# A tuned attention kernel: one check of the row sums in the last slots, simpler first loads, and quad 2 treated as any other

## The chip, the cores and the metric

One core of a Trainium2 chip runs the kernel. The metric is the device time of one execution in microseconds (us); the profile's span, from the first to the last instruction, is about 1.7 us shorter. Ratios in this document are computed as the mean time of one kernel's fast runs over the mean time of the other's fast runs of the same rounds, with a 95% interval, so they are not quite the ratios of the medians that stand beside them.

## The reference

```python
B, H, Sq, Sk, D = 16, 32, 192, 1024, 128          # bf16 inputs
scale  = q.shape[-1] ** -0.5
scores = jnp.einsum("bhqd,bhkd->bhqk", q, k) * scale
p      = softmax(scores, axis=-1)
out    = jnp.einsum("bhqk,bhkd->bhqd", p, v)
```

512 heads, each with 192 queries and 1024 keys. A "quad" is four heads; there are 128 quads, and a quad is worked on in three "fills" of the score banks, 384 fills (`NF`) in all.

## The kernel before

Each quad takes one load of K (1 MB), one of V (1 MB) and one of Q (192 KB), issued by SyncE into rings of five buffers. VectorE turns K and Q (the STREAM_TRANSPOSE rows; 0.97 us for one of K with 128x768), GpSimd reorders the turned K ("order", three pieces a quad) and spreads V beside a column of ones ("spread", two halves). TensorE computes a score block (`qk`) and, four fills later, an output block (`pv`). ScalarE takes exponentials, VectorE normalizes (`onorm`). The softmax takes no maximum: the row sums are checked against bounds, and where one is out of bounds everything is computed again on a general path (never here).

The loads at the start, on SyncE (cut):

```python
load_k(0)
e.wait_ge(s_blank, 1)
load_k(1); load_q(e, 1)
load_v(0, 0, 2)                       # half of V0
e.wait_ge(s_qk, PRE + 1)              # fill 0 is done
load_v(0, 2, 3); load_v(0, 3, 4)      # the other half, in two
load_k(2, 0, 8); load_k(2, 8, 16)     # half of K2, in two
e.wait_ge(s_qk, PRE + 2)              # fill 1 is done
load_k(2, 16, 24); load_k(2, 24, 32)
load_q(e, 2)
for n in range(3, NKN):               # V1, K3, Q3, V2, K4, Q4
    load_v(n - 2); load_k(n); load_q(e, n)
... # from here each load waits for its buffer
```

Quad 2 (`HELD = 2`) is treated apart: GpSimd orders its second piece of K before it spreads V1, so VectorE must hold the output block of fill 3 until V1's first half is spread:

```python
# GpSimd
order(3 * x)
if x == HELD: order(3 * x + 1)
if x >= 1:    spread(x - 1, 0); spread(x - 1, 1)
if x != HELD: order(3 * x + 1)
order(3 * x + 2)
# VectorE, end of onorm(s)
if s == 3 * (HELD - 1) - 1:
    ins.then_inc(s_held, 1); dve.wait_ge(s_held, 1)
    dve.wait_ge(s_vp, 2 * HELD - 1)
    dve.sem_inc(s_on, 1)
else:
    ins.then_inc(s_on if s < NF - 2 else s_fin, 1)
```

The check runs four times in the loop, over a quarter of the row sums each, in three parts (clamp, compare, reduce) behind three output steps; the last 24 columns are checked at the very end:

```python
PARTS = (0, NF // 4, NF // 2, 3 * NF // 4, NF - 12)
...
part = s - PARTS[i + 1] - 2
if 0 <= part < 3: check(i, part)
```

At the very end SyncE waits for the stores of all ten output buffers.

## Time and profile before

| | before |
|---|---|
| time, three runs | 813.84 us median, 812.44 to 814.58 |
| span of the profiled run | 810.3 us |
| TensorE busy | 799.4 us, 99% |
| ScalarE, VectorE, GpSimd busy | 93%, 74%, 68% |
| fill 0 starts, last fill starts | 8.75 us, 800.50 us |
| moved by the loads and stores | 319 MB, 394 GB/s on the mean |

In a timeline line stand the start and the duration in us, the engine, the source line, the operation with what it writes and reads, the shapes, how many were merged, and in brackets how long the engine idled before and what ended that. "issue" is a stop for which the profile shows no reason. PE is TensorE, DVE VectorE, ACT ScalarE, POOL GpSimd, SP SyncE. The lines that carry the argument stand in the prediction.

### The profile page before, as it was taken

The page shows a single profiled execution, that of the slowest core. Times are in us where ns is not written, and L with a number is a line of the kernel's source. Part 1 is how long each engine was busy: PE and PEld are TensorE (multiplying, and loading weights), DVE is VectorE, ACT ScalarE, POOL GpSimd, SP SyncE. Part 2 cuts the span into 40 slices and gives each one's busy share as a digit, 9 for nine tenths or more (in the row PEclk, how much of TensorE's full clock was granted, in tenths as well). Part 3 has the DMA queues.
Part 4 walks back from the last instruction along what each step waited for, and adds up shares of the span by engine and source line. Part 5 has one row for each costly group of instructions (what it writes and reads, how often), then busy time and mean ns, then how long its engine had stood idle before and what let it go on. Part 6 is the DMA issues. An engine that isn't in the chain of part 4 may idle for free. (4 is left out here: it accounts for less than half of the span.)

```text
span 810.3 us, 71469 instructions
## 1 busy us (share of the span) xinstructions
PE 799.4 (99%) x32996; PEld 713.3 (88%) x32996; DVE 602.5 (74%) x1301; ACT 749.9 (93%) x772; POOL 552.0 (68%) x648
## 2 busy tenths in 40 slices
PE   7999999999999999999999999999999999999998
PEld 5888888888888888888888888888888888888887
DVE  4677777777777777777777777777777777777775
ACT  5999999999999999999999999999999999999996
POOL 5676676677667667766766776676676667766763
PEclk9999999999999999999999999999999999999999
DMA  8999999999999999999999999999999999999994
GB/s 286 405 399 401 402 402 404 409 405 404 408 405 405 407 407 405 404 408 406 404 407 406 404 408 407 403 409 405 404 407 392 407 408 390 403 407 403 391 368 152
DMA packets 138904, 319.17 MB, mean 394 GB/s; under 512 B 7408, under 2 KB 56560, under 8 KB 122608
## 3 DMA queue, kind: packets, MB, share of 16 engines
q1 hardware_dynamic: 108048, 295.79, 93.3%
q10 hardware_dynamic: 30816, 23.01, 8.5%
q14 instruction: 34, 0.28, 0.1%
q8 instruction: 6, 0.10, 0.0%
HBM read 293.60 MB, written 25.17 MB: 393 GB/s over the span
## 5 line engine op out<-in xcount | busy, mean ns | idle before, releaser
L892 ACT ACTIVATE f_pt<-f_s 128x1536 bf16<-128x1536 f32 x384 | 554.6, 1444 | 0.0
L639 POOL COPY f_kt<-f_kx 128x768 uint32<-128x768 uint32 (+1 forms) x384 | 302.2, 788 | 240.3 <-DVE f_kx L783 240.1
L689 PE MATMUL f_s<-f_qt,f_kt 32*128 32x192 bf16 (+1 forms) x20528 | 422.0, 226 | 5.4 <-PEq L672 2.9
L718 PE MATMUL f_o<-f_vp,f_pt 128*64 128x129 bf16 x12368 | 425.9, 222 | 0.9 <-issue 0.9
L718 PEld LDWEIGHTS f_o<-f_vp,f_pt 128*64 128x64 bf16 x12368 | 362.4, 110 | 50.0 <-issue 23.0
L689 PEld LDWEIGHTS f_s<-f_qt,f_kt 32*128 32x128 bf16 x20528 | 348.0, 92 | 41.8 <-issue 6.5
L783 DVE STREAM_TRANSPOSE f_kx<-f_kn 128x768 uint32<-128x768 uint32 (+1 forms) x384 | 333.7, 870 | 9.3 <-DMA f_kn<-in_k_dram 9.1
L889 ACT ACTIVATE f_pt<-f_s 128x512 bf16<-128x512 f32 x384 | 229.3, 597 | 52.5 <-PE f_s L689 9.1
L648 POOL COPY f_vp<-f_vs 128x1024 uint32<-128x1024 uint32 x256 | 260.0, 1046 | 7.8 <-DMA f_vs<-in_v_dram 6.3
L821 DVE RECIPROCAL f_rinv<-f_o 128x2 f32<-128x2 f32 x381 | 64.7, 170 | 180.3 <-PE f_o L718 180.3
L827 DVE TENSOR_TENSOR f_ob<-f_o,f_rinv 128x256 bf16<-128x256 f32 x381 | 161.7, 424 | 13.0
L792 DVE STREAM_TRANSPOSE f_qt<-f_qn 128x384 uint32<-128x384 uint32 x128 | 72.8, 569 | 0.0
L876 ACT ACTIVATE f_pt<-f_ones 128x1536 f32<-128x1536 bf16 x3 | 4.2, 1471 | 0.0
L803 DVE TENSOR_SCALAR f_chk<-f_rinv 128x192 f32<-128x192 f32 (+2 forms) x5 | 3.9, 781 | 0.0
L627 POOL MEMSET f_vp<- 128x1088 uint32 (+1 forms) x3 | 3.8, 1311 | 0.0
L718 PE MATMUL f_s<-f_vp,f_pt 128*64 128x129 bf16 x96 | 3.1, 220 | 0.1
L718 PEld LDWEIGHTS f_s<-f_vp,f_pt 128*64 128x64 bf16 x96 | 2.8, 110 | 0.3 <-ACT f_pt L892 0.3
L805 DVE TENSOR_TENSOR f_chk<-f_chk,f_rinv 128x192 f32<-128x192 f32 (+1 forms) x4 | 2.8, 702 | 0.0
L876 ACT ACT_TABLE_LOAD x1 | 1.3, 1283 | 1.2 <-PEq L922 1.2
L731 PE MATMUL f_o<-f_ones 128*128 128x512 bf16 x2 | 1.0, 618 | 1.1 <-POOL f_ones L624 1.1
L756 DVE MEMSET f_pt<- 128x256 uint32 x4 | 1.1, 272 | 0.9 <-PEq L922 0.9
L821 DVE RECIPROCAL f_rinv<-f_s 128x2 f32<-128x2 f32 x3 | 0.5, 171 | 1.2 <-PE f_s L718 1.2
(16 smaller groups left out, 5.3 us busy)
## 6 DMA issues: line engine op xcount, KB each, us to landing
f_kn<-in_k_dram SPq DMA_DIRECT2D x127, 1024.0 KB, 17.9
f_vs<-in_v_dram SPq DMA_DIRECT2D x127, 1024.0 KB, 16.1
f_qn<-in_q_dram SPq DMA_DIRECT2D x127, 192.0 KB, 14.1
out_dram<-f_ob ACTq DMA_DIRECT2D x55, 384.0 KB, 9.5
out_dram<-f_ob SPq DMA_DIRECT2D x11, 192.0 KB, 5.7
out_dram<-f_ob ACTq DMA_DIRECT2D x6, 192.0 KB, 2.5
f_kn<-in_k_dram SPq DMA_DIRECT2D x4, 256.0 KB, 4.2
f_vs<-in_v_dram SPq DMA_DIRECT2D x1, 512.0 KB, 8.0
```

Of the source, the lines that this page charges most:

```text
L639: gp.tensor_copy(kt[:, x % NKT].bitcast(U32).rearrange("p U (j s u) c -> p U j s (u c)", s=2, u=2)[:, lo:hi], kx[:, x % 2].rearrange("p (U ...
L648: gp.tensor_copy(vp[:, x % NVP, 2 * T * i: 2 * T * i + 2 * T, 0:D].bitcast(U32), vs[:, x % NVS, 2 * i: 2 * i + 2, :].rearrange("p a (t d) ...
L689: ins = pe.matmul(S[:, c0: c0 + n1 - n0], kt[r, x % NKT, 2 * t + h, :, c], qt[r, x % R, h, n0:n1, c], start=w == 0 and g == 0, stop=w == 3 ...
L718: ins = pe.matmul(O[64 * z: 64 * z + 64, u, 0:129], pt[:, x % R, 2 * y + z, t * SQ + 64 * j: t * SQ + 64 * j + 64], vp[:, x % NVP, (2 * y ...
L783: dve.transpose(kx[:, x % 2].rearrange("p (U s j u) -> p s u U j", s=2, j=32, u=2)[:, :, :, lo:hi], kn[:, x % NKN].rearrange("p (s u U i) ...
L792: dve.transpose(qt[:, x % R].bitcast(U32).rearrange("p b (y j u) c -> p u y b (j c)", y=3, u=2), qn[:, x % NKN].rearrange("p (u y b i) -> ...
L803: ins = dve.tensor_scalar(c, rinv[:, lo:hi], 1.0 / RS_HI, 1.0 / RS_LO, ALU.max, ALU.min)
L821: dve.reciprocal(ri, O[:, :, 128]).then_inc(s_rc, 1)
L827: ins = dve.tensor_tensor(ob[:, so, 6 * a + 2 * w: 6 * a + 2 * w + 2, :], O[:, :, 0:128], ri.unsqueeze(2).to_broadcast([128, 2, D]), ALU.mult,
L876: return act.activation(part.bitcast(F32), ones[:, 0:1].to_broadcast([128, 2 * T * SQ // 2]), ACT_FN.Copy)
L889: act.activation(pt[:, x % R, 0, c], s1_ps[:], ACT_FN.Exp, scale=scale).then_inc(s_e1, 1)
L892: act.activation(pt[:, x % R, 1:4, c], s3_ps[f % 2][:], ACT_FN.Exp, scale=scale).then_inc(s_e3, 1)
```

## The change

The intent: take the four checks out of the loop, where each costs TensorE 0.42 to 0.45 us, and put one check between the last output steps; load with fewer and whole transfers (V0 without a wait, K2 behind fill 0, everything from Q2 and V1 on behind fill 2); and drop the special treatment of quad 2. Five of the ten waits for stores also move ahead of the last part of the program.

```diff
-    HELD = 2
-    PARTS = (0, NF // 4, NF // 2, 3 * NF // 4, NF - 12)
+    PARTS = (0, NF - 12)
 ...
+            late = [i % NSO for i in range(len(stores) - 5, len(stores))]
 ...
-                load_v(0, 0, 2)
+                load_v(0)
                 e.wait_ge(s_qk, PRE + 1)
-                load_v(0, 2, 3)
-                load_v(0, 3, 4)
-                load_k(2, 0, 8)
-                load_k(2, 8, 16)
-                e.wait_ge(s_qk, PRE + 2)
-                load_k(2, 16, 24)
-                load_k(2, 24, 32)
+                load_k(2)
+                e.wait_ge(s_qk, PRE + 3)
                 load_q(e, 2)
 ...
+                stored(e, [so for so in range(NSO) if so not in late])   # SyncE, ahead; the late ones as before at the end
 ...
-                    if x == HELD:
-                        order(3 * x + 1)
                     if x >= 1:
                         for i in range(2):
                             spread(x - 1, i)
                     if x < NQ:
-                        if x != HELD:
-                            order(3 * x + 1)
+                        order(3 * x + 1)
                         order(3 * x + 2)
 ...
-                    if s == 3 * (HELD - 1) - 1:
-                        ... # the hold
-                    else:
-                        ins.then_inc(s_on if s < NF - 2 else s_fin, 1)
+                    ins.then_inc(s_on if s < NF - 2 else s_fin, 1)
 ...
-                            part = s - PARTS[i + 1] - 2
+                            part = s - (NF - 5)
```

More of the change, by code (lines that the diff above doesn't have):

```diff
@@ L28, in _only_if, with _general_path @@
     return wrap
-def _general_path(nc, q, k, v, out, redo, hints, stored, G=16, NS=2, LAGS=(2, 4, 5, 7), ROUTES=(R_W, R_W, R_EA)):
+def _general_path(nc, q, k, v, out, redo, hints, stored, stored_late, G=16, NS=2, LAGS=(2, 4, 5, 7), ROUTES=(R_W, R_W, R_EA)):
     B, H, SQ, D = q.shape
@@ L195, in _ @@
             sync_general(e)
-            stored(e)
+            stored_late(e)
         @block.gpsimd
@@ L483, in _attention_kernel @@
         s_fin = sem("f_fin")
-        s_held = sem("f_held")
         s_fl = sem("f_fl")
@@ L567, in hint, with stored @@
                 hints[eng.engine] = eng.mark_branch_hint_location()
+            late = [i % NSO for i in range(len(stores) - 5, len(stores))]
+            def stored(e, sos=range(NSO)):
+                for so in sos:
+                    e.wait_ge(s_st[so], landed(so, len(stores)))
             @block.sync
@@ L617, in _ @@
                         store(e, i)
-            def stored(e):
-                for so in range(NSO):
-                    e.wait_ge(s_st[so], landed(so, len(stores)))
+                stored(e, [so for so in range(NSO) if so not in late])
             @block.gpsimd
@@ L645, in spread @@
                     if i == 0:
-                        gp.wait_ge(s_v[x % NVS], 16 * (x // NVS + (3 if x % NVS == 0 else 1)))
+                        gp.wait_ge(s_v[x % NVS], 16 * (x // NVS + 1))
                         gp.wait_ge(s_pv, 3 * (x - NVP) + 3 + BLANK)
@@ L779, in turn_k @@
                     if b == 0:
-                        dve.wait_ge(s_kn[x % NKN], 16 * (x // NKN + (4 if x % NKN == 2 else 1)))
+                        dve.wait_ge(s_kn[x % NKN], 16 * (x // NKN + 1))
                     if x >= 2:
@@ L832, in onorm @@
                     )
-                    if s == 3 * (HELD - 1) - 1:
-                        ins.then_inc(s_held, 1)
-                        dve.wait_ge(s_held, 1)
-                        dve.wait_ge(s_vp, 2 * HELD - 1)
-                        dve.sem_inc(s_on, 1)
-                    else:
-                        ins.then_inc(s_on if s < NF - 2 else s_fin, 1)
+                    ins.then_inc(s_on if s < NF - 2 else s_fin, 1)
                 turn_k(0)
@@ L896, in _ @@
                     store(act, i)
-        _general_path(nc, q, k, v, out, redo, hints, stored)
+        _general_path(nc, q, k, v, out, redo, hints, stored, lambda e: stored(e, late))
 def bass_standalone__mha_softmax__near_ridge_kernel(
```

## The prediction

> **What bounds the kernel now.** I read the page first (busy shares, slices, costliest groups), then the waits in total, then the timeline of the first 40 us, of one check in the middle, and of the last 30 us.
>
> ```profile
> span 810.3 us, 71469 instructions
> PE 799.4 (99%) x32996; PEld 713.3 (88%) x32996; DVE 602.5 (74%) x1301; ACT 749.9 (93%) x772; POOL 552.0 (68%) x648
> ...
> DVE f_rinv L821 <- PE f_o L718: 180.3, 373, 2.7
> ```
>
> TensorE is busy 99% and VectorE waits for it 373 times: between the ends of the program TensorE sets the pace. In the timeline its score fills start 2.05 us apart (785.71 to 787.77), each a score block and an output block of about 1.03 us. First fill 8.75 us, last fill 800.50: 791.75 us for 383 steps. At 2.054 us they would take 786.7, so about 5.1 us are lost inside the loop. Only this loss, and what lies before 8.75 and after 800.50, can change. Two places hold nearly all of it.
>
> First, the start (PE, DVE and POOL lines of the timeline):
>
> ```profile
> 8.75 1.10 PE L689 MATMUL f_s<-f_qt,f_kt 32*128 32x192 bf16 x48 [1.65 <-PEq L672]
> ...
> 11.83 0.93 PE L718 MATMUL f_o<-f_vp,f_pt 128*64 128x129 bf16 x26
> ...
> 13.40 0.36 PE L718 MATMUL f_o<-f_vp,f_pt 128*64 128x129 bf16 x6 [0.64 <-issue]
> ...
> 14.17 2.03 POOL L648 COPY f_vp<-f_vs 128x1024 uint32<-128x1024 uint32 x2 [2.19 <-DMA f_vs<-in_v_dram]
> ...
> 15.74 0.98 PE L689 MATMUL f_s<-f_qt,f_kt 32*128 32x192 bf16 x39
> ...
> 18.14 1.85 DVE L783 STREAM_TRANSPOSE f_kx<-f_kn 128x768 uint32<-128x768 uint32 x2 [5.17 <-DMA f_kn<-in_k_dram]
> ...
> 19.17 0.34 PE L689 MATMUL f_s<-f_qt,f_kt 32*128 32x128 bf16 x9 [2.45 <-issue]
> ```
>
> TensorE stops in the middle of a block twice, after 26 of 32 and after 39 of 48 matmuls, where no semaphore stands, and the releaser is "issue". Between the two stops lie 6+48+32+39 = 125 matmuls with as many weight loads, 250 instructions. The DMA view in narrow windows shows single packets of 0.02 MB on an "instruction" queue starting between 5.8 and 6.0, 10.8 and 11.0, 16.6 and 16.8, and 23.0 and 23.2. I read the two stops as waits for instruction blocks: 0.64 and 2.45 us. The six fills from 8.75 to 24.57 take 15.8 us instead of 12.3, so the start loses 3.5 us.
>
> Second, the four checks of the row sums. The first, on VectorE and TensorE:
>
> ```profile
> 224.41 0.94 DVE L803 TENSOR_SCALAR f_chk<-f_rinv 128x192 f32<-128x192 f32 x1
> ...
> 226.66 0.71 DVE L805 TENSOR_TENSOR f_chk<-f_chk,f_rinv 128x192 f32<-128x192 f32 x1
> ...
> 228.88 0.35 DVE L810 TENSOR_REDUCE f_bad<-f_chk 128x1 bf16<-128x192 f32 x1
> ...
> 228.31 1.10 PE L689 MATMUL f_s<-f_qt,f_kt 32*128 32x192 bf16 x48 [0.32 <-PEq L672]
> ```
>
> The fill before started at 225.81, so this step took 2.50 instead of 2.05 us. The other three checks show the same: 423.40 to 425.90, 620.99 to 623.48, 793.93 to 796.40. Excess 0.45+0.45+0.44+0.42, about 1.8 us with the hundredths beside them. The path is VectorE's: it falls behind and turns the next queries late.
>
> [...] the 192-column scalar operation takes 0.94 us beside GpSimd's copies and the 24-column one 0.18 us at the end where GpSimd is idle; the 168-column one ends at 793.45, 0.1 us after a GpSimd copy should end. [...]
>
> **The change part by part.**
>
> *Checks out of the loop.* All four go; TensorE gets 1.8 us back. In their place one check of 744 columns stands between the output steps of fills 379, 380 and 381, when VectorE has no more turning to do and GpSimd is idle (its last copy ends about 800.7). Durations, estimated from this trace: the scalar operation 0.18 + 720/2 x 1.04 ns = 0.55 us; the comparison 0.17 + 720 x 1.04 = 0.92; the reduce 0.35 + 552 x 1.04 = 0.92. The next operation can start about 0.08 us before each ends (a 0.42 us multiply is followed after 0.34). The end now:
>
> ```profile
> 802.87 0.42 DVE L827 TENSOR_TENSOR f_ob<-f_o,f_rinv 128x256 bf16<-128x256 f32 x1
> 803.57 0.17 DVE L821 RECIPROCAL f_rinv<-f_s 128x2 f32<-128x2 f32 x1 [0.28 <-PE f_s L718]
> ...
> 804.80 0.17 DVE L821 RECIPROCAL f_rinv<-f_s 128x2 f32<-128x2 f32 x1 [0.60 <-PE f_s L718]
> ...
> 806.62 0.17 DVE L821 RECIPROCAL f_rinv<-f_o 128x2 f32<-128x2 f32 x1 [0.28 <-PE f_o L718]
> ```
>
> On this clock: scalar operation 803.21; reciprocal 803.68 instead of 803.57; comparison 804.22; reciprocal 805.06 instead of 804.80; reduce 805.60; reciprocals 806.44 and 806.98, the last instead of 806.62. The last multiply, which releases the last store, comes 0.36 us later. TensorE's last block waits only for the multiply of fill 379, ahead of all this, so it isn't delayed. Cost 0.36 us, all on the path.
>
> *Waits for stores.* Five of the ten waits at the very end move ahead of it, into the flight of the last stores. From the last store's issue (807.35) plus its shortest landing (1.9 us) to 810.3 lie about 1.0 us, in which five satisfied waits run. I put the saving at 0.15 us; no row gives the time of one wait.
>
> *The start.* Work up to 8.75 us needs K0 and Q0 only: unchanged. Then it is a matter of when the two blocks arrive. From each packet's start to TensorE's going on I count 13.40 - 10.85 = 2.55 and 19.17 - 16.65 = 2.5 us. From entering a block (which I take as the request) to the packet's start: about 9.7 to 10.85 is 1.1 us with the loads nearly drained (94 GB/s at 10 to 11 us); 13.40 to 16.65 is 3.2 us with K2, Q2 and V1 queued. A block's matmuls run 3.3 us (13.40 to 16.72). So a fetch on a quiet queue costs 1.1+2.5-3.3 = 0.3 us, on a full one 2.4.
>
> After the change V0 comes whole, so the queue isn't quiet at 9.7: of the 3.55 MB of K0, Q0, K1, Q1 and V0 some 2.85 have moved, and 0.7 MB at 0.39 MB/us keep it busy until 11.5, with K2 following at about 11.3[...]. I choose the first packet at 12.0 instead of 10.85: TensorE goes on at 14.5 instead of 13.40, a loss of 1.1. Then K2, 1.05 MB, is through by about 14.2, and nothing more is issued until fill 2 ends (about 15.9). The second fetch, asked for at 14.5, meets a quiet queue: packet 15.6, TensorE on at 18.1 instead of 19.17. Net gain 1.1 us.
>
> *GpSimd and VectorE at quad 2.* With V1 issued at about 16.4, behind Q2, its bytes run from 17.8 to 20.4 and it lands near 21.3 (21.85 now). Spread 2.03 and order 0.86 us: K2's second piece is ready at 24.2. Fill 7 would start at 25.6. Slack 1.4 us, no cost. The hold removed from VectorE cost it 0.18 us of idle at 27.55 and TensorE nothing.
>
> Sum: 1.8 + 1.1 + 0.15 - 0.36 = 2.7 us. 813.84 - 2.7 = 811.1 us.
>
> **The rivals.** *The wait only moves.* If the first fetch meets the full 3.2 us, its packet starts at 12.9, TensorE goes on at 15.4, the second gives 19.0, and the start gains 0.2 us: 812.0. For it: V0 and K2 now follow without a hole. Against it: only 0.7 MB is left at the request. *Both stops nearly vanish.* If the first fetch isn't delayed by V0, TensorE goes on at 13.4 and, with the second quiet, at 17.0: gain 2.1 us, 810.1. *V1 too late.* If V1 lands over 1.4 us later than I work out, the second piece of K2 behind its spread holds up fill 7, microsecond for microsecond, and may eat the start's gain: 812 to 813. For it: the queue is idle from about 14 to 17 us, bytes that must be caught up at 404 GB/s of steady demand. *The end costs more.* [...] it takes 0.93 us and the end slips 0.75 instead of 0.36: 811.5.
>
> **Range and chances.** The sure parts are the checks (1.8) and the end (0.2 to 0.7 back); the start may give 0 to 2.1, a little less if V1 is late. That is 809.9 to 812.7 before the spread of the runs, which is 2.1 us over three of the kernel before. Range 808.9 to 813.4. Two per cent is 16 us, far more than all losses together (5.1 in the loop): faster by over 2% 0.01, within 2% 0.98, slower by over 2% 0.01.
>
> **What would show it.** In the changed profile: no L803 row of 192 columns, and steps of 2.05 us at fills 101 and 200; one row each of 744 columns near the end with 0.55, 0.92 and 0.92 us, the last reciprocal about 0.3 to 0.4 us after TensorE's last block frees it; the stop in the output block after fill 1 longer than 0.64 us (about 1.7), the one in fill 3 shorter than 2.45 (about 0.3); the wait of VectorE for K2 (5.17) gone. I am wrong if fill 7 waits for GpSimd, if TensorE's last block waits for VectorE, or if the stops don't follow the load on the queue.

The sum came to 1.8 + 1.1 + 0.15 - 0.36 = 2.7 us, so 811.1 us. What some of its numbers rest on is said here:

- The check's durations. In the trace of the kernel before a reduce takes 347 ns at 192 columns and 322 at 168, a comparison 708 and 683, so 1.04 ns a column for both; the scalar operation 935 and 924, so 0.46 ns a column, for which the 0.55 us has half of 1.04. In the changed kernel it takes 0.54 us at 744 columns and 0.18 at 24, so 0.50. In the rival "The end costs more", "it" is the scalar operation, supposed at 1.04 ns a column.
- The start of K2's and V1's bytes, at 11.3 and 17.8 us. The delay from issue to bytes that stands behind them was the author's estimate: the first packets of K0, issued at 0.81 us in the kernel before, start at 1.84.

## The result

| | before | changed |
|---|---|---|
| time, four runs each | 813.35 us median, 812.44 to 814.58 | 811.93 us median, 811.48 to 813.65 |
| ratio | | 0.9985, interval 0.9965 to 1.0006 |
| span of the profiled run | 810.3 us | 809.7 us |
| fill 0 starts | 8.75 us | 8.42 us |
| fill 9 starts | 30.74 us | 31.76 us |
| last fill starts | 800.50 us | 799.81 us |

The changed kernel is the same within 2%, and the four runs alone don't show that it is faster. The time lies in the range that was given; the sum of the steps does not hold, as the trace shows. First the start, on TensorE, GpSimd and VectorE (timeline of the changed kernel):

```profile
8.42 1.89 PE L682 MATMUL f_s<-f_qt,f_kt 32*128 32x192 bf16 x48 [2.44 <-PEq L665]
...
12.81 0.93 PE L711 MATMUL f_o<-f_vp,f_pt 128*64 128x129 bf16 x26
...
14.49 0.36 PE L711 MATMUL f_o<-f_vp,f_pt 128*64 128x129 bf16 x6 [0.76 <-issue]
...
16.83 0.98 PE L682 MATMUL f_s<-f_qt,f_kt 32*128 32x192 bf16 x39
...
18.34 0.34 PE L682 MATMUL f_s<-f_qt,f_kt 32*128 32x128 bf16 x9 [0.53 <-issue]
...
23.83 2.02 POOL L644 COPY f_vp<-f_vs 128x1024 uint32<-128x1024 uint32 x2 [5.46 <-DMA f_vs<-in_v_dram]
...
26.95 1.09 PE L682 MATMUL f_s<-f_qt,f_kt 32*128 32x64 bf16 x64 [1.05 <-PEq L665]
27.04 0.98 DVE L776 STREAM_TRANSPOSE f_kx<-f_kn 128x768 uint32<-128x768 uint32 x1 [2.53 <-DMA f_kn<-in_k_dram]
...
28.68 1.10 PE L711 MATMUL f_o<-f_vp,f_pt 128*64 128x129 bf16 x32 [0.63 <-PEq L665]
```

The second stop shrank from 2.45 to 0.53 us, nearly as forecast. But fill 0 took 1.89 us instead of 1.10, and behind fill 6 two new waits stand: fill 7 waits 1.05 us for GpSimd, which had waited 5.46 us for V1; and the output block behind it waits 0.63 us for VectorE, which had waited 2.53 us for K3. What was 0.81 us ahead of the kernel before at fill 6 (23.77 against 24.58) is 1.02 us behind at fill 9. The kernel before starts fill 7 without a wait:

```profile
24.58 1.10 PE L689 MATMUL f_s<-f_qt,f_kt 32*128 32x192 bf16 x48
...
26.64 1.09 PE L689 MATMUL f_s<-f_qt,f_kt 32*128 32x64 bf16 x64
```

The slow fill 0 has a plain reason in the view by stretches (columns: stretch, its length, busy time of TensorE, its weight loads, VectorE, ScalarE and GpSimd with instructions, granted TensorE clock, DMA share, GB/s):

```profile
9.00:10.00 1.00, 1.00 (x38) 1.00 (x31) 0.13 (x2) 0.00 (x0) 1.00 (x2) 0.50 0.96 370
```

```profile
9.00:10.00 1.00, 1.00 (x55) 0.89 (x46) 0.45 (x1) 0.10 (x1) 1.00 (x2) 1.00 0.98 380
```

The first line is the changed kernel, the second the kernel before: the clock was at half. The clock records put it at half from 7.94 to 11.35 us, 3.41 us. It is a matter of the run: another run of the same kernel, told at the end of the experiments, has the full clock up to its last 2 us. What brings such a stretch about is not shown; in the 3.41 us before 7.94 us TensorE was busy 1.45 us, 43% of the time.

Then the end:

```profile
802.51 0.54 DVE L796 TENSOR_SCALAR f_chk<-f_rinv 128x744 f32<-128x744 f32 x1
...
803.50 0.92 DVE L798 TENSOR_TENSOR f_chk<-f_chk,f_rinv 128x744 f32<-128x744 f32 x1
...
804.88 0.92 DVE L803 TENSOR_REDUCE f_bad<-f_chk 128x1 bf16<-128x744 f32 x1
...
806.25 0.16 DVE L814 RECIPROCAL f_rinv<-f_o 128x2 f32<-128x2 f32 x1
```

The durations are those of the prediction (0.55, 0.92 and 0.92). GpSimd's last copy ends at 799.98 us here; beside its copies, in the kernel before, the scalar operation took 0.94 us for 192 columns. The last reciprocal stands 0.37 us before that of the kernel before (806.62) where the last fill started 0.69 us earlier: the check gives 0.32 us back at the end. Between fill 9 and the last fill, 374 steps of 2.0537 us (nearly the changed kernel's own mean there) would take 768.1 us; the kernel before took 1.68 us more, the changed one 0.03 less. So the checks cost 1.71 us. From the last multiply's end to the end of the span it is 2.99 us before and 2.79 after, with the spans taken to the hundredth (810.32 and 809.74). The balance: 1.71 - 1.02 - 0.32 + 0.20 = 0.57 us; the spans differ by 0.58.

### The profile page after: what moved, and what is told of

Same layout as the page of the kernel before. It is cut to its first block, busy times and chain, and to the rows that moved or that the text cites. A ratio compares the mean times of both kernels' runs of the same rounds, so it can differ in the third digit from the quotient of the medians.

```text
span 809.7 us, 71454 instructions
## 1 busy us (share of the span) xinstructions
PE 799.3 (99%) x32996; PEld 713.4 (88%) x32996; DVE 598.8 (74%) x1292; ACT 749.9 (93%) x772; POOL 551.0 (68%) x648
## 4 chain that ended last, share of the span: by engine, by line
PE 96%; DVE 1%; issue 0%
PE f_o L711 48%; PE f_s L682 48%; DVE f_ob L820 0%; DVE f_bad L803 0%; DVE f_chk L796 0%; DVE f_rinv L814 0%; DVE f_chk L798 0%; DVE redo L853 0%; PE f_o L742 0%; DVE f_flag L798 0%; PE f_o L743 0%
```

## The experiments

A table first, from the records of all traces. "Lost" is the time from fill 9 to the last fill over 374 x 2.0537 us. "Lead" is how long a quad's K had landed when VectorE began to turn it, at quads 20, 60, 100 and 120, worked out from the landing records of the loads. "Clock" is the mean of the profiled run; 0.998 means one stretch of 3.41 us at half.

```
kernel               fill 9   last fill  lost    lead at 20 / 60 / 100 / 120   last K landed  span   clock
before                30.74    800.50    1.68     6.5    5.3    4.0    2.5     788.2          810.3  1.000
changed               31.76    799.81   -0.03     5.9    4.0    1.9    0.0     790.7          809.7  0.998
check_only            30.99    798.94   -0.13     7.1    5.0    2.7    0.6     789.2          809.2  1.000
start_only            30.48    803.27    4.71     4.7    2.7    0.4    0.0     793.8          813.1  1.000
waits_only            30.02    803.60    5.50     4.4    2.5    0.2    0.0     794.2          813.8  1.000
after_hold_kept       30.74    803.81    4.99     4.5    2.1    0.0    0.0     794.8          813.9  0.998
k3_first              34.44    802.48   -0.04    10.3    7.4    6.0    4.3     789.4          812.7  0.995
v0_split              29.79    799.84    1.97     5.4    2.9    0.0    0.0     790.9          809.8  0.998
no_second_wait        33.55    801.60   -0.03    13.0   11.9    8.4    6.7     786.6          811.5  0.998
best_try              30.65    801.23    2.50     5.9    3.6    0.5    0.0     792.2          810.8  0.998
before_half_stores    34.46    804.23    1.69    10.4   15.2   16.3   15.5     779.5          814.0  0.994
after_half_stores     31.36    799.42   -0.03     6.3   14.0   15.4   14.9     774.9          809.4  0.996
split_and_spread      29.99    798.70    0.63     5.5    3.0    0.2    0.0     789.6          808.9  0.998
changed_again         30.14    799.54    1.31     5.4    3.0    0.7    0.0     790.5          809.8  1.000
```

Two cautions. Every row is one execution, and the ones traced for start_only, waits_only and after_hold_kept were the slowest of their series, 1.8, 3.5 and 3.3 us above the median; what they lost after fill 9 is not typical of these kernels. And the start scatters: three traces with the unaltered start and the full clock took 21.99 (before), 22.56 (check_only) and 21.48 us (waits_only) from fill 0 to fill 9, two with the new start 21.92 (start_only) and 21.44 (changed_again). So one trace of each can't show a gain or loss of less than about 1 us at the start.

### check_only

```diff
-    PARTS = (0, NF // 4, NF // 2, 3 * NF // 4, NF - 12)
+    PARTS = (0, NF - 12)
-                            part = s - PARTS[i + 1] - 2
+                            part = s - (NF - 5)
```
on the kernel before.

> The kernel before with one change: one check of 744 columns between the output steps of fills 379 to 381 instead of four checks in the loop. Theory (the parts add up): TensorE no longer loses 0.45 us at each of four places, the last reciprocal comes about 0.32 us later than TensorE frees it, as in the changed kernel; so about 1.4 us faster than before (1.71 gained in the loop, 0.32 given back), all steps between fills near 101, 197, 293 and 379 at 2.05 us. Rival (the checks cost nothing because TensorE catches up, and the gain of the changed kernel is its start): the time equals before within 0.3 us.

Measured: 811.94 us median of six runs, before 813.03; ratio 0.9982, interval 0.9966 to 0.9998, so 1.5 us faster. "Lost" falls from 1.68 to -0.13 us. By the trace the rival (TensorE catches up after each check) is out. On the mean this part alone gives all that the whole change gives; its interval reaches from 0.2 to 2.8 us.

### start_only

The kernel before with the loads of the changed kernel, and quad 2 as any other; the checks and the waits stay.

> The kernel before with the loads, GpSimd's order and VectorE's release of the changed kernel; checks and waits at the end as before. Theory: the start is a loss. The second stop of TensorE (in fill 3) shrinks from 2.45 to about 0.5 us, but the first grows to about 1.5 us or more and fill 7 waits for GpSimd (V1 lands near 23.8 us), so fill 9 starts about 1 us later than the 30.74 us of before, and the kernel is 0 to 1.5 us slower than before. Rival (what the prediction held: the start gains 1.1 us): fill 9 starts before 30 us and the time is about 1 us below before.

```profile
14.03 0.36 PE L710 MATMUL f_o<-f_vp,f_pt 128*64 128x129 bf16 x6 [1.46 <-issue]
...
17.88 0.34 PE L681 MATMUL f_s<-f_qt,f_kt 32*128 32x128 bf16 x9 [0.53 <-issue]
...
25.61 1.10 PE L681 MATMUL f_s<-f_qt,f_kt 32*128 32x64 bf16 x64 [0.18 <-PEq L664]
25.77 0.98 DVE L775 STREAM_TRANSPOSE f_kx<-f_kn 128x768 uint32<-128x768 uint32 x1 [1.73 <-DMA f_kn<-in_k_dram]
...
27.41 1.10 PE L710 MATMUL f_o<-f_vp,f_pt 128*64 128x129 bf16 x32 [0.70 <-PEq L664]
```

Measured: 813.07 us against 813.03, ratio 0.9994, interval 0.9977 to 1.0011: no change. The first stop grew from 0.64 to 1.46 us and the second shrank to 0.53, as expected, and both waits behind fill 6 are there. But at full clock fill 9 starts 0.26 us sooner than before, neither 1 us later nor before 30 us as the rival had it, and that is within the scatter told under the table. I had taken the half clock of the changed kernel's first trace for a part of the change. And a loss that neither theory had stands further on: 4.71 us after fill 9, where the four checks explain 1.7 (in the slowest of the five executions).

### waits_only

```diff
-            stored(e)                  # all ten, last of all
+            stored_late(e)             # the last five; the other five stand ahead, behind the last store's issue
```
on the kernel before.

> The kernel before with one change: five of the ten waits for stores stand ahead of the last part. Theory: about 0.2 us less between the last multiply of VectorE and the end of the span (2.98 us before: 807.33 to 810.3; 2.74 in the changed kernel: 806.96 to 809.7), so 0.2 us in time, hardly to be told from noise. Rival (the 0.24 us are chance, a store that landed sooner): the distance stays at 2.9 to 3.0.

The last multiply and the span of this kernel:

```profile
810.61 0.42 DVE L831 TENSOR_TENSOR f_ob<-f_o,f_rinv 128x256 bf16<-128x256 f32 x1
```

```profile
span 813.8 us, 71469 instructions
```

Measured: from 811.03 to 813.83 (the span to the hundredth) it is 2.80 us. The four kernels without the moved waits have 2.99 or 3.00 us here (before, check_only, start_only, before_half_stores), the ten with them 2.79 or 2.80. So moving the five waits saves 0.2 us. In time it is lost in the spread: 812.09 against 813.03 us, ratio 0.9987, interval 0.997 to 1.0005.

### after_hold_kept

The changed kernel with the special treatment of quad 2 put back, as in the code of the kernel before.

> The changed kernel with the special treatment of quad 2 put back: GpSimd orders K2's second piece before it spreads V1, and VectorE holds the output block of fill 3 until V1's first half is spread. Theory (two waits side by side: fill 7 waits for GpSimd behind V1, and the output block after it waits for VectorE, which stands at K3's landing near 27.0 us): fill 7 starts about 1.1 us sooner (about 25.8), but the output block behind it still starts near 28.6 because of K3, so fills 8 and 9 stay where they are and the time equals the changed kernel's. Rival (the order on GpSimd is the only cause): fill 9 starts about 1.0 to 1.8 us sooner than the 31.76 us of the changed kernel, and so does the end.

```profile
25.10 1.09 PE L687 MATMUL f_s<-f_qt,f_kt 32*128 32x64 bf16 x64
...
25.93 0.98 DVE L781 STREAM_TRANSPOSE f_kx<-f_kn 128x768 uint32<-128x768 uint32 x1 [2.16 <-DMA f_kn<-in_k_dram]
...
27.66 1.10 PE L716 MATMUL f_o<-f_vp,f_pt 128*64 128x129 bf16 x32 [1.47 <-PEq L670]
```

Fill 7 starts without a wait, and the block behind it then waits 1.47 us for VectorE, which stands at K3. From fill 6 to fill 8 it takes 5.65 us, against 5.94 in the first trace of the changed kernel and 5.14 in start_only (4.11 without any wait). So dropping the special treatment is not what costs: the two late loads hold TensorE side by side. Time: 812.39 us, ratio to before 0.9989, interval 0.9972 to 1.0005.

### k3_first

```diff
-                for n in range(3, NKN):
+                load_k(3); load_v(1); load_q(e, 3)
+                for n in range(4, NKN):
```
on the changed kernel.

> The changed kernel with K3 issued ahead of V1 after fill 2. Theory (TensorE's loss behind fill 6 comes mostly from VectorE standing at K3): VectorE's wait for K3 (2.53 us in the changed kernel, 1.73 with the start alone) is gone, the output block behind fill 7 starts right behind it, and from the start of fill 6 to that of fill 8 it takes 4.1 to 4.9 us instead of 5.94; what is left of it is fill 7 waiting for GpSimd behind V1. Rival (V1 alone is the cause and K3's wait only shows in its shadow): V1 now lands later, fill 7 waits longer, and fill 6 to fill 8 takes 5.9 us or more.

```profile
25.65 2.02 POOL L647 COPY f_vp<-f_vs 128x1024 uint32<-128x1024 uint32 x2 [8.00 <-DMA f_vs<-in_v_dram]
...
28.77 1.10 PE L685 MATMUL f_s<-f_qt,f_kt 32*128 32x64 bf16 x64 [3.25 <-PEq L668]
```

My theory fell. VectorE no longer waits for K3, but V1 lands at 25.65 us and fill 7 waits 3.25 us; fill 6 to fill 8 takes 8.28 us, of which about 0.85 us is the half clock from 29.84 us on. 814.48 us, ratio 1.0008. K3's lateness was only the nearer of two waits; whichever of the two transfers comes second is too late. The load records say why both are late. In the changed kernel the queue is nearly empty at 15 to 17 us, and when it starts again it moves 0.02, 0.17, 0.20, 0.26, 0.33 and 0.30 MB in the six microseconds from 16 us on. With K3 first it is 0.17, 0.09, 0.24, 0.40 from 16 us on: the ramp is there whichever transfer comes first, though shorter with K3 first. My prediction had reckoned 0.4 MB/us for V1 from 17.8 us on, an estimate. A hole alone does not make such a ramp: v0_split, below, has one at 10 to 12 us (0.03 and 0.07 MB), and the next two microseconds move 0.33 and 0.45 MB. There V0's second half and K2 come behind the hole, here Q2 and then V1 or K3. Whether the hole or these loads make the ramp, no run takes apart.

### v0_split

```diff
-                load_v(0)
+                load_v(0, 0, 2)
                 e.wait_ge(s_qk, PRE + 1)
+                load_v(0, 2, 4)
                 load_k(2)
```
on the changed kernel (GpSimd counts the two transfers).

> The changed kernel with V0 in two halves again, the second behind fill 0 ahead of K2. Theory (a fetched block of instructions comes later the fuller the load queue is at its request): the first stop of TensorE, in the output block behind fill 1, shrinks to 0.4 to 0.7 us as in the kernel before (1.46 us with the start alone at full clock), since the queue runs dry near 10 us; the second stop, in fill 3, grows past 0.5 us, since K2 now ends about 1.3 us later. Rival (the stops follow the instruction count alone, not the queue): both stay where they are in the changed kernel.

```profile
15.91 0.98 PE L683 MATMUL f_s<-f_qt,f_kt 32*128 32x192 bf16 x39
...
18.22 0.34 PE L683 MATMUL f_s<-f_qt,f_kt 32*128 32x128 bf16 x9 [1.34 <-issue]
...
21.07 2.03 POOL L645 COPY f_vp<-f_vs 128x1024 uint32<-128x1024 uint32 x2 [2.75 <-DMA f_vs<-in_v_dram]
```

810.96 us against 813.89, ratio 0.9965, interval 0.9945 to 0.9984: 2.9 us faster than before. The first stop is gone altogether (fill 1 to fill 2 in 2.06 us), the second is 1.34 us, as the theory has it for a queue that is dry at the first request and full at the second. This trace has half clock from 8.08 to 11.50 us, which gives the first block more time (fill 0 to fill 1 in 3.48 us instead of 2.06), so the first stop is not a clean measure. And V1 lands 5.6 us after its issue instead of 7.5 (6.6 and 6.7 in start_only and changed_again): K2 was still on its way when V1 was issued. Even so the queue moved only 0.20, 0.29, 0.34 and 0.33 MB in the four microseconds from 16 us on, without having been empty. Fill 9 starts at 29.79 us in spite of the half clock, the soonest of all traces, but by no more than the scatter told under the table.

### no_second_wait

```diff
-                e.wait_ge(s_qk, PRE + 3)
```
on the changed kernel.

> The changed kernel without the wait for fill 2: Q2, V1 and all that follows is issued right behind K2. Theory: the queue is never empty between 10 and 20 us, so the second stop (in fill 3) grows from 0.5 to 2.4 us or more, V1 and K3 land 3 to 4 us sooner, and neither GpSimd at V1 nor VectorE at K3 holds TensorE behind fill 6 (fill 6 to fill 8 in 4.1 us). Fill 9 starts within 0.7 us of the changed kernel's place (31.76, or 30.5 at full clock), so the time is the same within 1 us. Rival (the loads' backlog does not matter to the block): the second stop stays near 0.5 and the kernel is 1.5 to 2 us faster than the changed one.

```profile
13.79 0.36 PE L710 MATMUL f_o<-f_vp,f_pt 128*64 128x129 bf16 x6 [1.19 <-issue]
...
20.68 0.49 PE L681 MATMUL f_s<-f_qt,f_kt 32*128 32x128 bf16 x9 [3.56 <-issue]
```

The queue is never empty (0.36 to 0.45 MB in every microsecond from 14 to 20), the second stop is 3.56 us, and fill 6 to fill 8 takes 4.11 us: the three expectations hold, and the rival is out. This is the cleanest evidence that the stop marked "issue" depends on the load queue: only a wait on SyncE was taken out, and it went from 0.53 (start_only, full clock) to 3.56 us. That it is a wait for instructions is inferred: in every trace that has such a stop TensorE goes on 2.2 to 3.3 us after a single packet of 16 KB on a queue of the kind "instruction" has started (10.95 and 16.77 us in the kernel before, 13.40 and 19.17 for TensorE). The pages count 6 packets on that queue (q8, 0.10 MB) in a whole span. But fill 9 starts at 33.55 us, 1.8 us behind the changed kernel's 31.76, where I had allowed 0.7: from the end of the longer stop on the clock was at half, from 20.3 to 23.7 us. 813.34 us, ratio 0.9992.

### best_try

The changed kernel with the special treatment of quad 2 and K3 ahead of V1, and the check spread where VectorE idles:

```diff
-                            part = s - (NF - 5)
-                            if 0 <= part < 3:
+                            part = {NF - 8: 0, NF - 6: 1, NF - 5: 2}.get(s, -1)
+                            if part >= 0:
```

> A version meant to beat both: the changed kernel with quad 2 treated apart as before, K3 issued ahead of V1, and the one check spread over the output steps of fills 376, 378 and 379, where VectorE idles 1.4 us a fill. Theory: fill 6 to fill 8 in 4.1 us, the last reciprocal within 0.05 us of TensorE's last block (the changed kernel gives 0.32 us away), so 1.5 to 2 us faster than the changed kernel in its span where no load is late further on: about 810 us, 2 to 3 below before. Rival (the loads set the end: they move 404 GB/s in nearly every slice, just what a quad every 6.16 us asks for): the time stays within 1 us of the changed kernel, with GpSimd and VectorE waiting for V and K in the second half of the run.

812.21 us, ratio 0.9977, interval 0.996 to 0.9995. The end is as the theory had it: the last reciprocal follows TensorE's last block without delay. The start is not: fill 6 to fill 8 takes 5.12 us, since V1 is late (25.69 us). And the rival is right about the rest: the lead of the loads goes from 5.9 us at quad 20 to nothing at quad 120, and 2.50 us are lost after fill 9 with no check in the loop.

### before_half_stores and after_half_stores

Both kernels with half of the stores left out, a wrong result:

```diff
                 for w, n in pieces(i):
+                    n = 1
                     e.dma_start(
```

> The kernel before, of each pair of quads only the first one's output is stored (a wrong result on purpose): 3.9% less to move, 2.39 instead of 2.49 MB a quad. Theory (the loads are a second bound: a quad's loads land 6.21 us apart while TensorE takes 6.16 us for it, so their lead over VectorE shrinks from about 6.5 us at quad 20 to 2.5 at quad 120, and in other runs to nothing): now the lead grows or stays, it is at least 6 us at quad 120, nothing waits for a load after 60 us, and the times of the runs lie within 1 us instead of the 4 us seen of the kernel before (811.8 to 816.1). Rival (the spread is the clock at the start or the chip): the spread stays above 2.5 us.

> The changed kernel with the same half of the stores left out. Theory: with the second bound out of the way, what the change itself does is left: 1.71 us gained at the checks, 0.32 given back at the end, 0.2 from the waits, the start 0 to 1 us worse. So 0.6 to 1.6 us faster than the kernel before with half its stores, with run times within 1.5 us. No step after fill 9 longer than 2.2 us. Rival (the change gains through the loads): the difference to the other kernel vanishes.

Both are needed to read the table. In the kernels with all stores, K of a quad lands 6.21 us (before: 123.4 at quad 20, 744.8 at quad 120) to 6.26 us (waits_only) after that of the quad before, and TensorE needs 3 x 2.0537 = 6.16 us for a quad. So the lead of the loads, some 5 to 7 us at quad 20, melts by 0.03 to 0.08 us a quad, and where it is gone before the end, the loads set the pace. With 3.9% less to move, the lead grows instead, to 15.5 and 14.9 us at quad 120, and the loss after fill 9 is just that of the checks: 1.69 and -0.03 us, a difference of 1.72. That part of the theory holds: the loads are a second bound, about 1% from the first (6.21 to 6.26 against 6.16 us a quad).

The other part fell: the spread of the run times did not shrink (811.2 to 816.6 us for before_half_stores where 1 us was expected, 809.7 to 812.6 for after_half_stores where it was 1.5). The rival is right about this. Its profiled run had the clock at half from 8.96 to 12.37 and from 19.20 to 26.02 us; the second stretch begins within this stop,

```profile
20.39 0.49 PE L690 MATMUL f_s<-f_qt,f_kt 32*128 32x128 bf16 x9 [3.25 <-issue]
```

and fill 9 started at 34.46 instead of 30.74 us. Of 44 timed runs of the kernel before, the 11 with a mean clock up to 0.995 took 814.4 us on the mean, the 9 with 0.999 or 1.000 took 812.4. So the start is also a lottery for the clock, worth some 2 us. The stops are only a part of it. In eight traces of the table the clock goes to half at 7.78 to 9.84 us, before either stop; what sets these apart is when the trace's record of the clock begins, at 4.37 to 6.43 us in these and at 6.63 to 7.62 in the other six. A later stretch at half, before the end, stands in three traces, where TensorE had waited 3.25 (before_half_stores), 3.56 (no_second_wait) and 3.25 us (k3_first); check_only waited 3.27 us without one. In the 3.41 us before each stretch at half that followed on full clock TensorE was busy 7 to 49% of the time (11 stretches).

The changed kernel with half the stores took 810.92 us, the kernel before with half the stores 813.22, 2.3 us apart (0.6 to 1.6 expected). Without the second bound the change is worth more, in part by the clock: 0.996 to 1.000 in its six runs, 0.994 to 0.999 in those of the other.

### split_and_spread

v0_split with the spread check of best_try.

> The changed kernel with V0 in two halves (the best so far, 2.9 us below before) and the one check spread over the output steps of fills 376, 378 and 379. Theory: the last multiply follows TensorE's last block without delay, 0.32 us less than v0_split from the last load to the end of the span (18.94 there, 18.6 in the other version with this check): about 810.6 where v0_split has 810.96, so 3.0 to 3.3 us below before. Rival (the check beside GpSimd's last copies holds VectorE up, as its four predecessors did): a step of 2.2 us or more near fill 381 and no gain.

```profile
804.51 0.17 DVE L815 RECIPROCAL f_rinv<-f_s 128x2 f32<-128x2 f32 x1 [0.28 <-PE f_s L712]
...
805.42 0.17 DVE L815 RECIPROCAL f_rinv<-f_o 128x2 f32<-128x2 f32 x1 [0.28 <-PE f_o L712]
```

810.92 us against 813.43, ratio 0.997, interval 0.9956 to 0.9984. VectorE now waits for TensorE before each of the last reciprocals, so the 0.32 us are no longer given away, and no step near fill 381 is long. In this span they don't show, since TensorE stops for 0.42 us ("issue") at 802.50: from the last fill to the end it is 10.23 us, 9.95 in v0_split. In time it can't be told from v0_split (810.96 in another call). It beats the kernel before by 2.5 us, where 3.0 to 3.3 were expected. Against the changed kernel (811.93 and 811.82) it was not timed side by side, so a gain over that one isn't shown. From the last K's landing to the end it is 19.3 us, not 18.6.

### changed_again

The changed kernel unaltered, timed again.

> The changed kernel unaltered, timed again, since its four runs leave the ratio between 0.9965 and 1.0006. Theory (1.7 us gained at the checks, 0.3 given back at the end, 0.2 from the waits, the start even or up to 1 us worse): 0.6 to 1.6 us below before, ratio 0.998 to 0.9993; in its trace again no step over 2.2 us between fill 9 and the last, fill 7 or the output block behind it late, and the slack of K's landing near 0 at quad 120. Rival (a gain near 2.7 us as predicted, and the four runs were unlucky): ratio 0.9975 or less.

811.82 us median (811.52 to 814.58), before 812.66; ratio 0.9996, interval 0.9981 to 1.0011. The prediction's sum of 2.7 us is out. This trace has full clock, and it is the fair comparison with that of the kernel before: fill 9 starts 0.60 us sooner (30.14 against 30.74), which is within the scatter told under the table. But now 1.31 us are lost after fill 9, in four steps above 0.15 us between 750 and 777 us, where I had expected no long step. The waits from 660 to 800 us name what is late (us in total, times, the longest):

```profile
POOL f_vp L644 <- DMA f_vs<-in_v_dram: 35.2, 21, 2.2
...
DVE f_kx L776 <- DMA f_kn<-in_k_dram: 8.6, 14, 1.1
```

The kernel before, in the same stretch, has no wait for a load at all; GpSimd waits for VectorE there:

```profile
POOL f_kt L639 <- DVE f_kx L783: 42.8, 45, 1.3
```

## Why the prediction was right or wrong

The forecast (the same within 2%, 811.1 us, range 808.9 to 813.4) held: 811.93 and 811.82 us were measured. That the number came so near is partly luck: by the ratios the gain was 1.2 and 0.3 us, where the sum had 2.7, and neither interval excludes that it is nothing. Step by step:

- **What bounds the kernel.** TensorE, right, but not alone. The page showed 404 GB/s in nearly every slice, and I used the figure only to say that a hole must be caught up. A comparison of 2.49 MB a quad at 404 GB/s (6.16 us) with three fills (6.16 us) was to be had before the change, and would have said that the gains can't simply be summed.
- **Checks out of the loop, 1.8 us.** Right: 1.71 us between the two traces, 1.72 between the two kernels with half the stores, and check_only is 1.5 us faster in time.
- **The end, 0.36 us back.** Right: 0.32 us, with the three operations at 0.54, 0.92 and 0.92 us.
- **Waits for stores, 0.15 us.** Right in kind, 0.2 us in size.
- **The start, 1.1 us gained.** This is the step that failed. Its first half held: TensorE went on at 14.49 and 18.34 us in the first trace, for 14.5 and 18.1 forecast, although the 14.49 came in part from the half clock (fill 0 took 1.89 us); at full clock the stops were 1.46 and 0.53 (start_only), 1.20 and 0.26 us (changed_again), for about 1.7 and 0.3. (The working's 0.3 us for a fetch on a quiet queue doesn't meet its own trace, which has 0.64: the block before that stop ran some 3.0 us, from about 9.7 to 12.76, not 3.3.) What failed is the line "its bytes run from 17.8 to 20.4 and it lands near 21.3": V1 was ready at 23.83 us in the first trace and near 22.5 in the next three, because the loads behind fill 2 took some four microseconds (three with K3 first) to come to their rate. The slack of 1.4 us at fill 7 became a wait, and I had not looked at K3 at all. The third rival ("V1 too late") had named this course. The net was -1.02 us at fill 9 in the first trace (in which fill 0 and the block behind it took 3.36 instead of 2.06 us, at half clock), +0.60 in the second, +0.26 with the start alone; with the scatter of the start, a gain is not shown.
- **The special treatment of quad 2.** The hold on VectorE cost nothing, as forecast (VectorE idles 0.18 us at 27.55 in the kernel before, and TensorE's blocks at 26.64, 27.66 and 28.69 follow without a stop), and putting it back gains little (after_hold_kept: 812.39 us).
- **What neither the sum nor the rivals had.** The loads as a second bound: where their lead was used up before the end, 0.6 to 5.0 us beyond the checks were lost again, from some 550 us on at the earliest (changed_again, start_only, waits_only, after_hold_kept, v0_split, best_try, split_and_spread). An early fill 9 alone does not say how much: before and after_hold_kept both have 30.74 us. And the clock at the start, a matter of the run, worth about 2 us between the runs of one and the same kernel.

What stays open: why the loads behind fill 2 come back to their rate so slowly, when those behind the hole of v0_split did not, and why the loads of one run come 6.21 and of another 6.26 us apart. No run here takes them apart.

## What to carry to other kernels

Before summing gains, compare the bytes of one step over the rate in the page with the step of the bounding engine. Here the two agreed (2.49 MB at 404 GB/s against three fills, 6.16 us each), and a gain on the engine was only kept as long as the loads had a lead to spend (2.5 us left at quad 120 in the kernel before, 0.0 in the changed one). Behind the wait that let the load queue run dry, the loads ran below their rate for three to four microseconds (0.02 to 0.26 MB a microsecond from 16 to 20 us in the changed kernel, 0.36 to 0.45 from 14 to 20 in no_second_wait); that the empty queue was the cause is not shown. What is behind the restart should be checked for every transfer, not only the first. And a single trace of a start is not the start: look at the granted clock there before reading a fill's length as an effect of the change (fill 0 took 1.89 us at half clock, 1.10 at full).
